# Two scheduling rules for VectorE's banks and polynomial steps, and one multiplication in place of two, in a two-block attention kernel

## The chip, the cores and the metric

One core of a Trainium2 chip (trn2). The metric is the device time of one execution in microseconds (us), lower is better. Each execution also comes with the mean clock that TensorE was granted, as a share of full speed. A run is called slow when it lies over 1.5% above the fastest of its kernel, and such runs are left out of ratios, means and clocks. Ratios are the mean time of one kernel's fast runs over that of the other's fast runs of the same rounds, so not quite the ratio of the medians quoted beside them.

## The reference

Two attention blocks over 2048 positions, 32 heads of 16 channels, laid side by side in the output. Block A attends to everything, block B to a causal window of 256.

```python
qkv = (x @ wqkv).reshape(B, S, 3, H, Dh)...          # S = 2048, H = 32, Dh = 16
scores = jnp.einsum("bhqd,bhkd->bhqk", q, k) * (Dh ** -0.5)
# block B only: scores = where(0 <= i - j < 256, scores, -1e9)
p = _softmax(scores, axis=-1)
o = jnp.einsum("bhqk,bhkd->bhqd", p, v)
return o... @ wo                                     # a and b concatenated
```

## The kernel before

The program is unrolled in Python into 743 slots. A slot is three banks of scores (three 128 x 512 tiles), which ScalarE turns into probabilities in one instruction. Two sets of three banks take turns; one bank (`op`) accumulates the values and one (`ms`) serves everything else: projections, guards, outputs and "polynomial" scores. These last are scores whose exponential VectorE computes, to take them from ScalarE: a copy of the bank (`dy`), then, for each two banks, three steps of 1024 columns.

```python
    def poly_ok(self, key):
        at = self.landed.get(key[:2] + (key[2] // 2,))
        return (at is not None and at <= self.slot and len(self.dq) < 4
                and self.slot >= self.last_poly + 1)
...
    # in poly_steps: one bank
            b = self.bank()
            ... matmul of scores into b ...
            nc.vector.tensor_copy(out=y[:, half, :], in_=b[:])          # L622
            self.queued(OP, True)
            self.closed = self.last_poly = self.slot
    ...     # after the second bank of a pair
            self.dq += [first, second, third]                           # L633, L637, L643
```

The loop over slots. `self.vec` is the time at which VectorE's queue ends by the program's own reckoning; `whole` counts the pieces of TensorE work put into the slot, and what is lacking of two is made up by `busy`, matmuls of the identity into the score bank before the scores overwrite it:

```python
        for s, sl in enumerate(slots):
            self.slot = s
            self.exps(sl)
            if self.dq and self.by(self.vec, 0.8):
                self.queued(1.22, at=0)
                self.dq.pop(0)()
            if s + 2 < len(slots):
                self.scores(slots[s + 2])
            self.values()
            ...
            self.whole = 0
            ... a guard (whole = 1), a polynomial bank (+ 1), other tasks (+ 2) ...

    def scores(self, slot):
        ...
            if b == 0 and jb.inst == 0:
                self.busy(sps[:, 0, :], 2 - self.whole)

    def busy(self, bank, n):
        for _ in range(n):
            self.nc.tensor.matmul(bank, lhsT=self.ident[:], rhs=self.junk, start=True, stop=True)
```

The last two units of block A (a unit is four heads over 512 positions) are normalised without a trip through memory: reciprocals of the sums are spread over 32 rows by matmuls with a one-row operand, then multiplied.

```python
        def spread(w):
            b = self.bank()
            for q in (slice(q, q + w) for q in range(q0, q1, w)):
                for j in range(GH):
                    r = slice(32 * j, 32 * j + 1)
                    nc.tensor.matmul(b[32 * j:32 * j + 32, q], lhsT=self.ones[r, 0:32],
                                     rhs=rec[r, q], start=True, stop=True,
                                     tile_position=(32 * j, 32 * j))         # L717
                nc.vector.tensor_mul(out=o[:, q], in0=osb[:, q], in1=b[:, q])  # L720
                self.queued(OP * w / 512, True)
```

## Time and profile before

| | before |
|---|---|
| median of the first 3 runs | 1049.49 us (1048.85 to 1050.01) |
| span of the profiled run, mean clock | 1048.8 us, 0.987 |
| ScalarE's exponentials (L590): busy, idle before them | 998.1 us, 22.3 us |
| TensorE busy | 935.5 us, 200.7 of it filler (L156) |
| half-clock stretches between the first and the last exponential | 3.4 us at 142, 10.2 us at 657, 6.8 us at 1019 |

How to read it: ScalarE has something to do in every slot, so its idle time is all that a better order can win. The prediction shows the lines.

### The profile page before, as it was taken

The numbers are of one execution on the slowest core, as the hardware profiler recorded it, in microseconds if no ns is written. First come the engines' busy times: TensorE is split into PE (matmuls) and PEld (weight loads), VectorE is DVE, ScalarE is ACT, GpSimd is POOL, SyncE is SP. The second block draws the span as 40 slices with busy tenths as digits, with TensorE's granted clock in tenths as the row PEclk, the third lists the DMA queues.
The fourth block names the chain that finished last, engine by engine and source line by source line (L and its number), as shares of the span: only waits on it lengthen the run. The fifth ranks groups of instructions, "written<-read, shape, count | busy, mean of one in ns | idle before, by whom it ended". The sixth has DMA issues, their size and how long they took to land.

```text
span 1048.8 us, 18724 instructions
## 1 busy us (share of the span) xinstructions
PE 935.5 (89%) x7653; PEld 317.6 (30%) x7653; DVE 722.3 (69%) x943; ACT 1008.3 (96%) x775; POOL 20.1 (2%) x100
## 2 busy tenths in 40 slices
PE   8888788888899989999998999999999999998887
PEld 5322222232233323333322333233222332323322
DVE  4432265537867977788788767877877768587754
ACT  5999999999999999999999999899999999999996
POOL 6000000000000000000000000000000000000000
PEclk9999999999999999999999999899999999999998
DMA  7021431112232103211230312123102211221101
GB/s 242 6 82 37 134 114 46 54 65 78 72 83 78 63 26 94 72 63 43 81 104 26 96 61 76 47 80 88 65 32 84 73 57 61 79 73 42 51 13 42
DMA packets 72359, 73.05 MB, mean 70 GB/s; under 512 B 22584, under 2 KB 55888, under 8 KB 72272
## 3 DMA queue, kind: packets, MB, share of 16 engines
q1 hardware_dynamic: 69216, 68.01, 21.0%
q0 software_dynamic: 768, 2.13, 0.5%
q10 hardware_dynamic: 2288, 1.70, 0.5%
q8 instruction: 60, 0.98, 0.4%
q14 instruction: 27, 0.22, 0.1%
HBM read 38.65 MB, written 31.07 MB: 66 GB/s over the span
## 4 chain that ended last, share of the span: by engine, by line
ACT 58%; PE 23%; issue 11%; DVE 7%; DMA 1%; ACTq 0%; DVEq 0%
ACT pT L590 58%; PE sps L563 5%; PE op L682 4%; PE ms L252 4%; PE sps L156 4%; PE ms L619 2%; PE sps L572 2%; DVE dy L622 2%; DVE dh L633 1%; DVE pD L643 1%; DMA kTa<-in_A_x_dram 1%; DVE dh L637 1%; DVE kst L270 0%; PE op L252 0%; PE sps L830 0%
## 5 line engine op out<-in xcount | busy, mean ns | idle before, releaser
L590 ACT ACTIVATE pT<-sps 128x1536 bf16<-128x1536 f32 (+3 forms) x759 | 998.1, 1470 | 22.3 <-PE sps L563 17.9
L563 PE MATMUL sps<-qTa,kTa 32*128 32x512 bf16 (+1 forms) x1904 | 248.7, 380 | 8.7 <-ACT pT L590 7.5
L156 PE MATMUL sps<-ident 128*128 128x512 bf16 x608 | 200.7, 383 | 54.7 <-ACT pT L590 47.9
L622 DVE COPY dy<-ms 128x512 f32<-128x512 f32 x204 | 139.9, 686 | 117.2 <-PE ms L619 116.4
L682 PE MATMUL op<-pT,va 128*32 128x512 bf16 (+1 forms) x1904 | 188.5, 386 | 0.8 <-ACT pT L590 0.6
L563 PEld LDWEIGHTS <-kTa 32*128 32x128 bf16 x1904 | 65.6, 91 | 237.2 <-issue 235.6
L633 DVE SCALAR_TENSOR_TENSOR dh<-dy 128x1024 f32<-128x1024 uint16 x102 | 124.6, 1222 | 2.8
L637 DVE SCALAR_TENSOR_TENSOR dh<-dy,dh 128x1024 f32<-128x1024 uint16 x102 | 124.0, 1215 | 1.5
L643 DVE SCALAR_TENSOR_TENSOR pD<-dh,dy 128x1024 uint16<-128x1024 f32 x102 | 124.0, 1216 | 1.0
L156 PEld LDWEIGHTS <-ident 128*128 128x128 bf16 x608 | 55.2, 96 | 166.5 <-issue 160.4
L619 PE MATMUL ms<-qTa,kTa 32*128 32x512 bf16 (+1 forms) x208 | 78.0, 378 | 11.2 <-DVE dy L622 2.8
L682 PEld LDWEIGHTS <-va 128*32 128x32 bf16 x2112 | 51.3, 93 | 106.1 <-issue 104.1
L572 PE MATMUL sps<-mask,ident 128*128 128x128 bf16 (+1 forms) x640 | 77.8, 248 | 0.0
L563 PE MATMUL sps<-qTb,kTb 32*128 32x384 bf16 (+2 forms) x704 | 56.1, 274 | 16.2 <-ACT pT L590 14.2
L759 DVE COPY osb<-op 128x512 f32<-128x512 f32 x62 | 42.5, 685 | 23.1 <-PE op L682 23.0
L572 PEld LDWEIGHTS <-ident 128*128 128x128 bf16 x640 | 43.6, 97 | 31.9 <-issue 29.2
L376 DVE TENSOR_SCALAR qs<-ms 128x512 bf16<-128x512 f32 x31 | 21.3, 689 | 37.8 <-PE ms L252 37.4
L270 DVE CAST kst<-ms 128x512 bf16<-128x512 f32 x28 | 19.3, 689 | 35.6 <-PE ms L252 35.2
L252 PE MATMUL ms<-wv,xT 128*128 128x368 bf16 (+2 forms) x176 | 37.7, 318 | 1.1 <-DVE qs L376 0.5
L563 PEld LDWEIGHTS <-kTb 32*128 32x128 bf16 x704 | 24.7, 92 | 42.0 <-issue 36.8
L252 PE MATMUL ms<-xT,wq 128*128 128x512 bf16 x124 | 35.4, 382 | 1.9 <-DVE dy L622 1.2
L682 PE MATMUL op<-pT,vb 128*32 128x384 bf16 (+2 forms) x704 | 36.6, 280 | 0.5 <-DVE osb L759 0.2
(105 smaller groups left out, 421.9 us busy)
## 6 DMA issues: line engine op xcount, KB each, us to landing
od<-osb SPq DMA_DIRECT2D x62, 256.0 KB
oc<-od SPq DMA_DIRECT2D x31, 256.0 KB
rb<-rd SPq DMA_DIRECT2D x31, 256.0 KB
kTb<-kd SPq DMA_DIRECT2D x16, 256.0 KB
qTb<-qd SPq DMA_DIRECT2D x16, 256.0 KB
qd<-qs SPq DMA_DIRECT2D x31, 128.0 KB
out_dram<-ob SPq DMA_DIRECT2D x31, 128.0 KB
qTa<-qd SPq DMA_DIRECT2D x15, 256.0 KB
```

The lines of the kernel that those rows point to most:

```text
L156: self.nc.tensor.matmul(bank, lhsT=self.ident[:], rhs=self.junk, start=True, stop=True)
L252: self.nc.tensor.matmul(bank, lhsT=lhs(c), rhs=rhs(c), start=(c == 0), stop=(c == NC - 1))
L563: self.nc.tensor.matmul(sps[:, b, o:o + q1 - q0], lhsT=kT[r, gg, k0:k0 + P], rhs=qT[r, gg, q0:q1], start=(o == jb.subs[0][3]), stop=not jb ...
L572: self.nc.tensor.matmul(sps[:, b, o:o + P * len(kind)], lhsT=self.ident[:], rhs=m, start=False, stop=True, skip_group_check=True)
L590: nc.scalar.activation(out=pT[:, b:e, :n], in_=sps[:, b:e, :n], func=ACT.Exp, scale=LN2 / 128, bias=-127 * LN2)
L619: nc.tensor.matmul(b[:, o:o + q1 - q0], lhsT=kT[r, g % 2, k0:k0 + P], rhs=self.qT[0, p, g // 2][r, g % 2, q0:q1], start=True, stop=True, t ...
L622: nc.vector.tensor_copy(out=y[:, half, :], in_=b[:])
L633: nc.vector.scalar_tensor_tensor(out=st["h"][:], in0=low, scalar=-65536.0, in1=low, op0=ALU.add, op1=ALU.mult)
L637: nc.vector.scalar_tensor_tensor(out=st["h"][:], in0=low, scalar=65536.0 * POLY[1], in1=st["h"][:], op0=ALU.add, op1=ALU.mult)
L643: nc.vector.scalar_tensor_tensor(out=out.bitcast(U16), in0=st["h"][:], scalar=POLY[0] * 2.0 ** -41, in1=flat, op0=ALU.mult, op1=ALU.add)
L682: self.nc.tensor.matmul(op[32 * jb.j:32 * jb.j + 32, q0:q1], lhsT=self.v[jb.inst, kt][:, h * VP:h * VP + 32], rhs=jb.pT[:, o:o + q1 - q0], ...
L759: nc.vector.tensor_copy(out=osb[:], in_=self.op[i, p, g][:])
```

## The change

The intent: banks for VectorE at least two slots apart, steps only when its queue is short, and one multiplication of 512 columns instead of two of 256 in the last unit but one.

```diff
-                and self.slot >= self.last_poly + 1)
+                and self.slot >= self.last_poly + 2)
...
                     nc.tensor.matmul(b[32 * j:32 * j + 32, q], lhsT=self.ones[r, 0:32],
                                      rhs=rec[r, q], start=True, stop=True,
                                      tile_position=(32 * j, 32 * j))
+                if self.mid:
+                    nc.vector.tensor_mul(out=o[:, q], in0=osb[:, q], in1=b[:, q])
+            if not self.mid:
+                q = slice(q0, q1)
                 nc.vector.tensor_mul(out=o[:, q], in0=osb[:, q], in1=b[:, q])
-                self.queued(OP * w / 512, True)
+                self.queued(OP, True)
...
-            if self.dq and self.by(self.vec, 0.8):
+            if self.dq and self.by(self.vec, 0.4):
```

## The prediction

> **What bounds the kernel now.** I read the page's busy shares first, then the groups of instructions, then who waited for whom, then the rows of ScalarE in order of time, and last the stretches in which ScalarE stood still.
>
> ```profile
> PE 935.5 (89%) x7653; PEld 317.6 (30%) x7653; DVE 722.3 (69%) x943; ACT 1008.3 (96%) x775; POOL 20.1 (2%) x100
> PEclk9999999999999999999999999899999999999998
> L590 ACT ACTIVATE pT<-sps 128x1536 bf16<-128x1536 f32 (+3 forms) x759 | 998.1, 1470 | 22.3 <-PE sps L563 17.9
> L156 PE MATMUL sps<-ident 128*128 128x512 bf16 x608 | 200.7, 383 | 54.7 <-ACT pT L590 47.9
> L622 DVE COPY dy<-ms 128x512 f32<-128x512 f32 x204 | 139.9, 686 | 117.2 <-PE ms L619 116.4
> L633 DVE SCALAR_TENSOR_TENSOR dh<-dy 128x1024 f32<-128x1024 uint16 x102 | 124.6, 1222 | 2.8
> ```
>
> ScalarE is the bound: the exponentials of L590 alone cover 998.1 of the 1048.8 us and wait only 22.3 us in all. The kernel runs in slots of one exponential; most start 1.33 to 1.34 us after the one before. The change takes no work from ScalarE: in the built program it has 784 instructions before and after. So everything that can be won lies in those 22.3 us, and in the head (21 us until the first exponential) and the tail (7.8 us after the last), which the change hardly touches. TensorE's 89% is padded: L156 is filler that nobody reads, put in where a slot has less than two other pieces of work.
>
> The 22.3 us, row by row in time (my sorting, by what stands just before each wait): 2.7 us in the first 56 us; 9.9 us in or just behind three stretches in which TensorE's clock was halved (1.8 at 142 us, 3.8 at 657 us, 4.4 at 1019 us); 4.6 us in 19 waits with a wait of TensorE for a bank of VectorE within 2.8 us before; 2.9 us in slots with mask matmuls; some 2 us of others. The last of the clock stretches, at the end, shows the mechanism at its largest:
>
> ```profile
> 1016.42 0.69 DVE L622 COPY dy<-ms 128x512 f32<-128x512 f32 x1 [1.62 <-PE ms L619]
> 1017.14 1.22 DVE L633 SCALAR_TENSOR_TENSOR dh<-dy 128x1024 f32<-128x1024 uint16 x1
> 1017.31 0.63 PE L717 MATMUL ms<-oc,padneg 1*32 1x256 f32 x8
> 1018.28 0.41 DVE L720 TENSOR_TENSOR oTa<-osb,ms 128x256 bf16<-128x256 f32 x1
> 1018.75 0.78 PE L717 MATMUL ms<-oc,padneg 1*32 1x256 f32 x8 [0.81 <-DVE oTa L720]
> ...
> 1020.73 1.45 ACT L590 ACTIVATE pT<-sps 128x1536 bf16<-128x1536 f32 x1 [1.96 <-PE sps L563]
> ```
>
> Columns: start, duration, engine, line; in brackets the idle time before and who ended it. The first half of the spreading matmuls (L717) is done, its multiplication stands behind a 1.22 us polynomial step, the second half waits 0.81 us for that multiplication, the scores behind it come late, and ScalarE stands for 1.96 us. Then the clock:
>
> ```profile
> 1015.70:1019.10 3.40, 2.59 (x44) 0.84 (x41) 2.25 (x3) 3.07 (x3) 0.00 (x0) 1.00 0.02 5
> 1019.10:1025.90 6.80, 6.80 (x47) 1.59 (x43) 2.75 (x4) 2.90 (x2) 0.00 (x0) 0.50 0.06 19
> ```
>
> (Stretch, length, busy time of PE, PEld, DVE, ACT, POOL, clock, DMA share, GB/s.) After a stretch with TensorE busy for 2.59 of 3.40 us, the clock is 0.50 for 6.8 us, and ScalarE is busy for only 2.90 of them.
>
> **What the Trainium skill says.** "TensorE: Matmul & The Clock Gate", section "What's actually happening": a monitor halves TensorE's clock after an idle window of about 3.4 us and restores it after a busy one. The trace agrees on the step (0.50) and the lengths (the three stretches are 3.4, 10.2 and 6.8 us); but TensorE was not idle before them, only less busy (2.40 of 3.50, 2.64 of 3.40, 2.59 of 3.40 us), and other windows as thin passed. "PSUM — Partial Sum Buffer", "PSUM bank collisions raise a hardware error": guard by bank, not by address. That is why the second half of the spread waits for the multiplication of the first, though the columns differ (0.81 us above). "VectorE: DVE Perf Modes", "The perf-mode tier table", gives an fp32 operand in PSUM one element a cycle; L622 takes 686 ns for 512, so one 512-wide multiplication should cost about what L788 takes (some 680 ns) against 0.41 + 0.42 us for two halves. The same engine's queue is in order (the TensorE page, "Architectural detail"); the trace shows it: L720 behind L633.
>
> **The change, part by part.**
>
> 1. A polynomial bank at most every second slot. The number of banks is fixed (208 matmuls of L619, 204 copies of L622, before and after), so no work goes. In the two built programs' order I counted the distances, in slots, between slots with such a bank: 53 of 203 were 1 before, none after; 2 goes from 49 to 85. Where two banks fall in neighbouring slots the second matmul, or the projection after it, waits for a 0.69 us copy that may stand behind a 1.22 us step. At 232.9, 391.8 and 868.1 us TensorE so waits 0.84, 0.85 and 0.58 us, and ScalarE then 0.74, 0.54 and 0.41 us. Of the 4.6 us in bank waits I take half, **-2.3 us**; the other half follows copies of keys, queries and outputs, which the rule does not space.
>
> 2. A polynomial step only if VectorE's modelled queue ends by 0.4 of the slot, not 0.8. It removes no instruction (306 steps of about 1.22 us). It keeps long steps from piling up before a bank's copy, but delays results. The order does not show harm: matmuls of L682 that run a slot later than usual fall from 55 to 25. I book it in part 1, **0**.
>
> 3. One multiplication after all eight spreading matmuls in the last unit but one. Saved on VectorE: 0.83 - 0.68 = 0.15 us, off the path. What counts is the 0.81 us wait in the middle of the spread, and that in the new order the multiplication stands before the polynomial step, not behind it. Without the pause the spread lasts about 1 us from 1017.31, then a filler: scores begin near 1018.6 instead of 1020.0, and ScalarE, which was ready at 1018.77, waits some 0.3 instead of 1.96 us. That is -1.4 to -1.6 us. If the window is then full enough that the clock stays up, the waits of 0.92 and 1.48 us behind it shrink too; but two groups of four output matmuls still stand in the way, so I count -3.2 us in all then. At 6 to 4 for the clock staying up: 0.6 x 3.2 + 0.4 x 1.4 = **-2.5 us**.
>
> 4. A side effect: fillers fall from 608 to 579, since slots with a bank and a projection together need none. That is 29 x 0.21 us = 6 us of TensorE time (0.21 us is the step between two fillers in the timeline). It is no gain, as TensorE isn't the bound; it makes thin windows a little likelier. The two middle clock stretches cost 5.6 us now; I add **+0.5 us**.
>
> Sum: -2.3 + 0 - 2.5 + 0.5 = -4.3 us, 1049.49 - 4.3 = **1045.2 us**.
>
> **The rivals.** (a) *Nothing moves.* ScalarE is 96% busy and each bank wait removed is met by another: the new order moves 208 banks to other slots, and some fall beside mask slots. For it speaks that only 4.6 us are at stake in the middle; against it the plain chain at 1018 us. It would give 1048 to 1049.5 us. (b) *The clock decides.* With fewer fillers a further window or two drops to half clock: 3.4 us of it cost ScalarE about 1.8 us at 142 us, 10.2 us cost 3.8. For it speaks that the count of fillers falls and TensorE's weighted work with it by 1.1%; against, that the end gets denser. Two more stretches give 1049 to 1051 us; losing the middle ones too gives 1040 us. (c) *Polynomial results come late*, the accumulation of a unit must wait for them, and VectorE's chain becomes the bound at the ends of units. The lag count (55 to 25) speaks against it; it would give 1052 us or more.
>
> **Range and chances.** The three runs of before lie within 1.2 us, so the range is that of the model: (a) at the top, the good side of (b) at the bottom: 1041.5 to 1049.3 us. Faster by over 2% needs -21 us, nearly all of the 22.3 us: 0.01. Slower by over 2% needs (c) in full: 0.01. The rest, 0.98, is within 2%.
>
> **What would show each step right or wrong.** Part 3: the eight L717 matmuls follow each other with no wait in the middle, and ScalarE's wait behind them is under 1 us. Part 1: TensorE's waits for L622 (4.4 us in 10 waits among the matmuls into these banks) fall by half or more, and L590's idle time falls from 22.3 to 16 to 19 us, L590's busy time staying within 2 us of 998. Part 4: the half-clock stretches between 100 and 1000 us number two, give or take one. The prediction is wrong if the waits for banks fall and L590's idle time does not, or if clock stretches come or go by more than one.

## The result, and the profile after

The changed kernel took 1040.97 us (median of 4 runs, 1039.03 to 1042.57), against 1049.17 us for the kernel before (4 runs): ratio 0.9921, 95% interval 0.9897 to 0.9944. That is "same" at 2%, as forecast, but twice the predicted gain and just outside the range. The page of the changed kernel:

```profile
PE 907.8 (87%) x7537; PEld 313.1 (30%) x7624; DVE 722.8 (69%) x942; ACT 1007.2 (97%) x775; POOL 20.1 (2%) x100
PEclk9999999999999999999999999999999999998999
...
L590 ACT ACTIVATE pT<-sps 128x1536 bf16<-128x1536 f32 (+3 forms) x759 | 997.0, 1486 | 15.2 <-PE sps L563 10.6
L156 PE MATMUL sps<-ident 128*128 128x512 bf16 x579 | 191.1, 382 | 60.8 <-ACT pT L590 52.2
L622 DVE COPY dy<-ms 128x512 f32<-128x512 f32 x204 | 139.9, 686 | 109.2 <-PE ms L619 107.4
```

(The trace lacks the records of 87 projection matmuls, 7537 against 7624 weight loads, so PE's 907.8 us is too low; e4_both_rules below, whose trace has them all, shows 921.4 us.)

The span is 1040.9 us, 7.9 less. L590's idle time fell by 7.1 us, from 22.3 to 15.2; its busy time by 1.1. So the gain is where it had to be. But sorting its waits as in the prediction gives: start 2.7 us as before; bank waits 4.1 (4.6 before); slots with mask matmuls 3.5 (2.9); others 2.3 (1.8); in or behind half-clock stretches 2.1 (9.9). The banks gave almost nothing; nearly all lies in and behind the clock stretches. Not all of that is the clock's own: the 1.96 us wait of the old spread is in it, of which the prediction put 1.4 to 1.6 us down to the pause in the spread. TensorE's waits for L622's banks did fall, from 4.4 to 2.7 us, but those for the copy of keys (L270) rose from 2.4 to 5.1 us, so together they did not fall. Before and after, TensorE's idle time ahead of a matmul into these banks, by who ended it (us, times):

```profile
  DVE dy L622: 4.4, 10
  DVE kst L270: 2.4, 5
...
  DVE kst L270: 5.1, 10
  DVE dy L622: 2.7, 9
```

The spread at the end, in order of time (columns as in the prediction):

```profile
1011.80 0.69 DVE L622 COPY dy<-ms 128x512 f32<-128x512 f32 x1 [1.58 <-PE ms L619]
...
1012.69 1.07 PE L717 MATMUL ms<-oc,padneg 1*32 1x256 f32 x16
...
1013.83 0.69 DVE L724 TENSOR_TENSOR oTa<-osb,ms 128x512 bf16<-128x512 f32 x1 [1.33 <-PE ms L717]
...
1014.43 1.22 DVE L633 SCALAR_TENSOR_TENSOR dh<-dy 128x1024 f32<-128x1024 uint16 x1
1014.53 2.96 ACT L590 ACTIVATE pT<-sps 128x1536 bf16<-128x1536 f32 x2 [0.37 <-PE sps L563]
```

The eight spreading matmuls (16 records) run through in 1.07 us, the multiplication stands before the polynomial step, and ScalarE waits 0.37 us instead of 1.96. The stretches around it, and around the only half-clock stretch that this profile has in the middle:

```profile
944.40:947.80 3.40, 2.26 (x31) 0.79 (x23) 3.01 (x4) 3.40 (x4) 0.00 (x0) 1.00 0.30 101
947.80:954.60 6.80, 6.80 (x38) 1.24 (x36) 3.65 (x4) 5.06 (x4) 0.00 (x0) 0.50 0.14 48
...
1011.40:1014.80 3.40, 3.25 (x45) 1.26 (x43) 1.66 (x3) 3.03 (x4) 0.00 (x0) 1.00 0.02 5
```

With the spread at 1012 us TensorE is busy for 3.25 of 3.40 us and keeps its clock. A thin window at 944 us (2.26 of 3.40) costs 6.8 us of half clock. Of the four runs, two with clocks of 0.995 and 0.997 took 1042.5 us each, two with 0.999 took 1039.0 and 1039.5 us.

**Theory:** the gain is TensorE's clock. A 3.4 us window in which the array does too little is followed by half clock; the scores come late and ScalarE waits. The change fills or moves the thin windows. **Rival:** the gain is the shorter waits for VectorE's banks, and the clock stretches of the two profiles are chance.

### The profile page after: what moved, and what is told of

The parts are those of the page before. It is cut to its first block, busy times and chain, and to the rows that moved or that the text cites. A ratio compares the mean times of both kernels' runs of the same rounds, so it can differ in the third digit from the quotient of the medians.

```text
span 1040.9 us, 18590 instructions
## 1 busy us (share of the span) xinstructions
PE 907.8 (87%) x7537; PEld 313.1 (30%) x7624; DVE 722.8 (69%) x942; ACT 1007.2 (97%) x775; POOL 20.1 (2%) x100
## 4 chain that ended last, share of the span: by engine, by line
ACT 62%; PE 18%; issue 12%; DVE 6%; DMA 1%; ACTq 0%; DVEq 0%
ACT pT L590 62%; PE sps L563 4%; PE ms L252 4%; PE op L682 3%; PE sps L156 3%; PE sps L572 2%; PE ms L619 1%; DVE dy L622 1%; DVE dh L633 1%; DMA kTa<-in_A_x_dram 1%; DVE dh L637 1%; DVE qs L376 0%; DVE ob L421 0%; DVE pD L643 0%; DVE osb L763 0%
## 5 line engine op out<-in xcount | busy, mean ns | idle before, releaser
L590 ACT ACTIVATE pT<-sps 128x1536 bf16<-128x1536 f32 (+3 forms) x759 | 997.0, 1486 | 15.2 <-PE sps L563 10.6
L156 PE MATMUL sps<-ident 128*128 128x512 bf16 x579 | 191.1, 382 | 60.8 <-ACT pT L590 52.2
L622 DVE COPY dy<-ms 128x512 f32<-128x512 f32 x204 | 139.9, 686 | 109.2 <-PE ms L619 107.4
L682 PE MATMUL op<-pT,va 128*32 128x512 bf16 (+1 forms) x1904 | 185.3, 383 | 0.0
L682 PEld LDWEIGHTS <-va 128*32 128x32 bf16 x2112 | 50.6, 93 | 105.0 <-issue 104.1
L563 PE MATMUL sps<-qTb,kTb 32*128 32x384 bf16 (+2 forms) x704 | 56.2, 273 | 17.1 <-ACT pT L590 14.2
L270 DVE CAST kst<-ms 128x512 bf16<-128x512 f32 x28 | 19.3, 690 | 38.6 <-PE ms L252 38.1
L252 PE MATMUL ms<-wv,xT 128*128 128x368 bf16 (+2 forms) x161 | 34.8, 313 | 1.9 <-DVE dy L622 0.7
L345 DVE CAST va<-ms 128x368 bf16<-128x368 f32 (+1 forms) x28 | 11.8, 441 | 32.8 <-PE ms L252 32.8
```

What stands on the lines that cost most here:

```text
L252: self.nc.tensor.matmul(bank, lhsT=lhs(c), rhs=rhs(c), start=(c == 0), stop=(c == NC - 1))
L563: self.nc.tensor.matmul(sps[:, b, o:o + q1 - q0], lhsT=kT[r, gg, k0:k0 + P], rhs=qT[r, gg, q0:q1], start=(o == jb.subs[0][3]), stop=not jb ...
L590: nc.scalar.activation(out=pT[:, b:e, :n], in_=sps[:, b:e, :n], func=ACT.Exp, scale=LN2 / 128, bias=-127 * LN2)
L682: self.nc.tensor.matmul(op[32 * jb.j:32 * jb.j + 32, q0:q1], lhsT=self.v[jb.inst, kt][:, h * VP:h * VP + 32], rhs=jb.pT[:, o:o + q1 - q0], ...
```

## The experiments

All outputs are right. "Clock" is the mean over a kernel's fast runs. The four groups of rounds had before at 1048.17, 1049.11, 1049.62 and 1049.21 us (medians of 11 runs each). Medians are over all runs: c4_few_fillers has one slow run (1106.41 us) and before in the third group another (1058.69 us); without them the medians are 1085.23 and 1049.25 us.

| run | what | median us | clock | ratio to before, 95% interval |
|---|---|---|---|---|
| e1_spacing | bank rule alone | 1049.68 | 0.9855 | 1.0023 (0.9998 to 1.0048) |
| e2_queue | queue rule alone | 1048.19 | 0.9860 | 1.0009 (0.9976 to 1.0043) |
| e3_spread | spread alone | 1045.94 | 0.9913 | 0.9990 (0.9966 to 1.0015) |
| e4_both_rules | both rules, old spread | 1043.37 | 0.9938 | 0.9958 (0.9935 to 0.9981) |
| a2_after_again | the changed kernel | 1040.40 | 0.9965 | 0.9924 (0.9883 to 0.9964) |
| c4_few_fillers | changed, fewer fillers | 1085.52 | 0.8696 | 1.0353 (1.0306 to 1.0399) |
| c2_two_holes | changed, 16 fillers out | 1046.54 | 0.9822 | 1.0000 (0.9934 to 1.0067) |
| c1_two_patches | before, 9 fillers in | 1045.46 | 0.9950 | 0.9955 (0.9936 to 0.9974) |
| d4_before_filled | before, 152 fillers in | 1053.82 | 0.9937 | 1.0049 (1.0006 to 1.0093) |
| d3_after_filled | changed, 142 fillers in | 1046.72 | 0.9983 | 0.9984 (0.9940 to 1.0028) |
| d1_loads_uncounted | changed, 12 fillers in | 1040.74 | 0.9960 | 0.9929 (0.9880 to 0.9977) |

### The parts one by one

e1_spacing: only the bank rule.

```diff
-                and self.slot >= self.last_poly + 1)
+                and self.slot >= self.last_poly + 2)
```

> The kernel before with only the bank rule (two slots apart). Clock theory (the gain of 8 us is that TensorE's clock is no longer halved at 142, 657 and 1019 us, and those stretches cost ScalarE 9.9 us of waits): the stretch at 1019 us stays, as the spread is untouched, and costs some 4 us; whether the two in the middle go depends on how full the moved slots are, so 1041 to 1050 us, and in the profile L590's idle time is 12 us plus what lies in half-clock stretches. Rival (waits for VectorE's banks are the gain): 1043 to 1045 us, with TensorE's waits for L622 well below the 4.4 us of before.

Measured: no gain (1.0023). Its profile has half clock at 301 us (3.4 us), 728 us (13.7 us) and 1018 us (6.8 us); 11 us of L590's 22.3 us of idle time lie outside them and the few us behind. TensorE's waits for L622's banks fell all the same, from 4.4 to 2.6 us, as in the changed kernel. The bank rival, which wanted 1043 to 1045 us from this rule, fails. The stretch at 728 us has a cause of its own. The windows before and in it (columns as before), and TensorE's wait in the timeline:

```profile
724.20:727.60 3.40, 1.64 (x16) 0.43 (x13) 2.95 (x4) 3.08 (x3) 0.00 (x0) 1.00 0.90 200
727.60:741.30 13.70, 12.36 (x51) 2.15 (x51) 7.85 (x10) 7.92 (x6) 0.00 (x0) 0.50 0.35 107
```

```profile
722.88 2.16 SPq L241 DMA_TRANSPOSE xT<-in_B_x_dram  x1
...
728.70 0.61 PE L252 MATMUL ms<-xT,wk 128*128 128x512 bf16 x1 [2.87 <-DMA xT<-in_B_x_dram]
```

The rule moved the projection of keys closer to the transposed load of its input: it starts 5.8 us after the load is issued, the wait included, against 8.8 us in the kernel before. TensorE waited 2.87 us for the transfer; that emptied the window. ScalarE was then busy for 7.92 of 13.70 us.

e2_queue: only the queue rule.

```diff
-            if self.dq and self.by(self.vec, 0.8):
+            if self.dq and self.by(self.vec, 0.4):
```

> The kernel before with only the tighter rule for polynomial steps (0.4 of a slot for 0.8). Clock theory: as for the run with the bank rule alone, the stretch at 1019 us stays; fillers fall from 608 to 590 but values lag less, so slots are filled more evenly: 1043 to 1048 us, half-clock stretches in the middle none or one. Bank rival: near 1049 us, as neighbouring banks stay (51 of 203 distances are 1).

Measured: no gain (1.0009), clock 0.9860, a miss for my hope that the middle would have none or one: the profile has 3.4 us at 142, 10.2 us at 667 and 3.4 us at 773, and the one at 1019 us (3.4 us). It speaks against the bank rival once more: TensorE's waits for L622's banks nearly doubled, from 4.4 to 8.4 us, and the time stayed.

e3_spread: only the third hunk of the change, the rest as before.

> The kernel before with only the multiplication after all eight spreading matmuls. The order of everything before 1008 us is the kernel before's, so the stretches at 142 and 657 us should be there again. Clock theory: the stretch at 1019 us goes, ScalarE's waits behind the spread fall from 4.4 to about 0.7 us, as in the changed kernel: 1045.3 us, -3.6. Bank rival, which counts only the 0.81 us pause and the late multiplication: -1.5 us, 1047.7 us, with the clock still at 0.50 around 1019 us.

Measured: 1045.94 us, ratio 0.9990 with an interval that includes 1, so the predicted 3.6 us are not resolved in the times; the difference of the means, -1.4 us, lies nearer to the rival's -1.5, and the mean clock (0.9913) is hardly above that of before in the same rounds (0.9905). The profile shows the point itself: no half clock around the spread, and ScalarE's waits behind it are 1.0 us, not 4.4. And it shows something that I had not expected: the order before 1008 us is that of the kernel before, yet the stretches at 142 and 657 us are not there; one at 970 us is. So where the clock drops differs from execution to execution of the same order.

e4_both_rules: both rules, the old spread.

> The changed kernel with the old spread in two halves: both scheduling rules, not the third part. Clock theory: the middle as in the changed kernel (none or one short stretch), the stretch at the end back: 1041 + 3.6 = 1044.6 us. If the parts add, this and the run of the spread alone sum to -8.2 us.

Measured: 1043.37 us, ratio 0.9958: a clear gain where each rule alone had none. Half clock at 98 us (3.4 us) and, as expected, behind the old spread at 1013 us (6.8 us). By the means this is -4.1 us, with e3_spread's -1.4 in all -5.5 where the expectation had -8.2; the intervals are too wide to say that the parts do not add.

a2_after_again: the changed kernel once more.

> The changed kernel again, to have it on the same chip and in the same rounds. Clock theory: about 1041 us, mean clock about 0.997, every run on the line 1039.1 us + 0.70 us for each 0.001 under full clock within 1 us. Against the runs of before of these rounds: some 5 to 7 us faster.

Measured: 1040.40 us, ratio 0.9924, as the first time. Its profiled execution had no half clock at all between the first and the last exponential, and took 1039.16 us.

### Is it the clock?

Every run has a time and a mean clock. For the 44 fast runs of the kernel before whose clock is listed (1042.4 to 1057.0 us, clock 0.998 to 0.979; one slow run of 1058.69 us is left out) the two correlate at -0.98. One line through these and the ten runs of the changed kernel, with one slope, gives 0.70 us for each 0.001 of mean clock (some 2.1 us at half clock), and at full clock 1041.0 us for before and 1038.4 us for after. The slope is that of before: the ten runs of the changed kernel alone, with clocks of 0.994 to 1.000, give 0.39 us and correlate at only -0.60. A line is not yet a cause, so fillers were taken out and put in.

c4_few_fillers: one filler fewer in each slot.

```diff
-                self.busy(sps[:, 0, :], 2 - self.whole)
+                self.busy(sps[:, 0, :], 1 - self.whole)
```

> The changed kernel with one filler fewer in every slot (187 for 579); all other instructions and their order the same. Clock theory, from the runs so far (a line through all runs of six kernels: 0.70 us for each 0.001 that the mean clock lies under 1, about 1039 us at full clock for the changed kernel): TensorE is thinner everywhere, the mean clock falls to 0.97 or less, and the time rises along that line, to over 1055 us. If fillers only take TensorE's time and the clock does not matter, it is equal or some us faster, 1038 to 1041 us.

Measured: 1085.52 us. From its page, the clock in 40 slices and the exponentials:

```profile
PEclk9998889897768789987899988889888999887768
...
L590 ACT ACTIVATE pT<-sps 128x1536 bf16<-128x1536 f32 (+3 forms) x759 | 1005.2, 1468 | 50.6 <-PE sps L563 38.5
```

Work that nobody reads was taken away, and the kernel lost 45 us against the changed one: L590's idle time went from 15.2 to 50.6 us. The direction is settled. The size is not on the line (0.13 under full clock would be 91 us). That half clock costs less where fewer fillers fill TensorE would explain it, but no run shows it.

c2_two_holes: fillers out in two short places.

```diff
-                self.busy(sps[:, 0, :], 2 - self.whole)
+                n = 2 - self.whole if not 353 <= self.row <= 360 and not 538 <= self.row <= 544 else 0
+                self.busy(sps[:, 0, :], n)
```

(`row` counts the calls of `scores`.)

> The changed kernel with 16 fillers taken out of 579 in two places, slots 353 to 360 (near 500 us) and 538 to 544 (near 750 us), where no run so far had a half-clock stretch. Clock theory: half-clock stretches appear at both places, each of 3.4 to 10.2 us, ScalarE waits 1 to 4 us at each, mean clock falls by 0.003 to 0.010, time rises by 2 to 7 us to 1043 to 1047 us, though TensorE has 3.4 us less to do. Without the clock theory: no change, or a little faster.

Measured: 1046.54 us, clock 0.9822 (4 runs, 1043.0 to 1056.5). The two places in its profile:

```profile
496.50:499.90 3.40, 2.21 (x20) 0.67 (x18) 2.97 (x5) 3.40 (x4) 0.00 (x0) 1.00 0.17 45
499.90:510.10 10.20, 9.03 (x52) 1.78 (x48) 6.12 (x9) 9.46 (x8) 0.00 (x0) 0.50 0.18 54
...
752.50:769.60 17.10, 16.45 (x75) 2.84 (x74) 10.56 (x12) 13.92 (x11) 0.00 (x0) 0.50 0.04 15
```

and the same two stretches of the unpatched changed kernel (a2_after_again):

```profile
499.90:510.10 10.20, 9.34 (x78) 3.05 (x77) 7.02 (x12) 10.20 (x8) 0.00 (x0) 1.00 0.20 64
...
752.50:769.60 17.10, 15.12 (x108) 4.39 (x107) 14.62 (x16) 17.10 (x14) 0.00 (x0) 1.00 0.00 1
```

Half clock came at the two holes, 10.2 and 17.1 us long, and ScalarE lost 0.7 and 3.2 us in them, while with the fillers it was busy throughout. (17.1 us is longer than I had expected.) The place near 500 us is a weaker witness: d1_loads_uncounted, below, has 6.8 us of half clock there without a hole. Near 752 to 769 us no other trace has half clock, c4_few_fillers aside. The fair comparison in time is that d1, in the same rounds, took 1040.8 us (mean) at a clock of 0.9960; c2's four runs have a mean of 1048.2 us at 0.9822.

c1_two_patches: the kernel before, nine fillers more in two places where its traces had half clock.

```diff
-                self.busy(sps[:, 0, :], 2 - self.whole)
+                n = 2 - self.whole + (self.row in (85, 86, 87, 88, 465, 466, 467, 468, 469, 470))
+                self.busy(sps[:, 0, :], n)
```

> The kernel before with nine fillers more (617 for 608), in slots 85 to 88 and 465 to 470, where its half-clock stretches at 142 us and at 656 us (two of three traces, 10.2 us each) begin. Clock theory: both places stay at full clock; with 656 us tripping in some two of three executions, the mean half-clock time falls by about 7 us, the mean clock rises by 0.003 and the time falls by some 2 us against before of the same rounds. If the place does not matter, the time is that of before.

Measured: 1045.46 us, ratio 0.9955, clock 0.9950 against 0.9876 for before in the same rounds. Both places keep their clock in its one profile (which has 3.4 us each at 129, 231 and 1017 us):

```profile
138.40:145.30 6.90, 6.42 (x42) 1.97 (x41) 4.81 (x7) 6.70 (x6) 0.00 (x0) 1.00 0.38 124
650.00:667.50 17.50, 16.47 (x135) 5.13 (x131) 15.80 (x19) 17.28 (x14) 0.00 (x0) 1.00 0.21 69
```

Nine matmuls that compute nothing won 4.2 us (by the means), as much as both scheduling rules together. No bank, step or spread was moved. So the clock alone can give what the rules gave. That is twice what I had expected (some 2 us and 0.003 of clock, measured 0.0074): more than the two places account for, and why is open. That the rules themselves work through the clock rests on e1 and e2, where waits for banks fell or doubled and the time stayed, and on e4_both_rules's clock (0.9938 against 0.9905 for before, by the slope 2.4 of its 4.1 us).

### More fillers everywhere

d4_before_filled and d3_after_filled: fillers also in slots whose task only starts a transfer, and one more after a slot without values.

```diff
-        self.whole += 1 if t["name"][0] == "d" else 2
+        self.whole += {"d": 1, "w": 0, "x": 0, "wo": 0, "ends": 0}.get(t["name"][0], 2)
...
-                self.busy(sps[:, 0, :], 2 - self.whole)
+                self.busy(sps[:, 0, :], 2 - self.whole + (self.valued < self.slot))
```

(`valued` is the slot after the last one with values.)

> The kernel before, its schedule of banks, polynomial steps and spread untouched, with fillers where it skipped them for nothing: tasks that only start a transfer no longer count as TensorE work, and a slot whose values group was empty gets one filler more (760 for 608). Clock theory: the mean clock rises to 0.995 or more and the time falls to 1041 to 1044 us, most of the change's gain without the change; the stretch at the end, behind the old spread, stays in most runs. If the change's gain is its own scheduling, it stays at 1048 us or gets slower by up to the 152 x 0.21 = 32 us of added TensorE work where that does not fit.

> The changed kernel with the same two filler rules (721 for 579). Clock theory: clock 0.998 or more in all runs, 1039 to 1040 us, a little faster than the changed kernel and with less spread; if the added 142 x 0.21 = 30 us of TensorE work do not fit into its waits, some us slower at a high clock.

Measured: both miss. The clock did rise, from 0.989 to 0.994 and from 0.997 to 0.998, but the times rose too, to 1053.82 and 1046.72 us. The page of d3_after_filled has full clock, and yet the exponentials are busy for longer and wait longer than in a2_after_again (996.3 and 14.1 us there):

```profile
PE 933.0 (89%) x7679; PEld 318.6 (30%) x7766; DVE 722.6 (69%) x942; ACT 1010.7 (97%) x775; POOL 20.1 (2%) x100
PEclk9999999999999999999999999999999999999999
...
L591 ACT ACTIVATE pT<-sps 128x1536 bf16<-128x1536 f32 (+3 forms) x759 | 1000.6, 1452 | 17.1 <-PE sps L564 11.2
```

Fillers are not free where a slot is full already. Taken to full clock by the slope, d3 is some 7.1 us above the changed kernel for 142 fillers, d4 some 8.2 us above before for 152: about 0.05 us each, an estimate from these means. Few in the right place help; many everywhere cost.

d1_loads_uncounted: the first of the two filler rules alone, on the changed kernel.

> The changed kernel with only this rule: a task that does nothing but start transfers (weights, inputs, the last rows of wo) no longer counts as TensorE work, so that its slot gets its fillers (591 for 579). It aims at the one half-clock stretch in the profile of the changed kernel (947.8 us), which begins just after the task that loads the last rows of wo. Clock theory: that place no longer trips, mean clock 0.998 or more, 1039 to 1040 us, about 1 us under the changed kernel. If twelve fillers are too little to tell: 1040.5 us, as the changed kernel.

Measured: 1040.74 us, clock 0.9960: no difference from the changed kernel. In its profile the stretch at 948 us is gone, and one of 6.8 us stands at 500 us. So the place at 948 us was mended and the clock did not gain: the expected 0.998 was missed. No version beat the changed kernel clearly.

### Second and third traces

b2_before_look and b3_before_look: the kernel before, unchanged, one look each.

> The kernel before, unchanged, for a second trace of it. Clock theory with windows that run free of the kernel: the half-clock stretches are not at 142 and 657 us again but at other thin places (or some of the same), while the one at 1015 to 1026 us, behind the spread, comes again in most executions. If they belong to fixed places of the program: 142, 657 and 1019 us again, to 2 us.

> The kernel before, unchanged, for a third trace, with the same expectations as the second: by the clock theory, other middle places than in the first two traces, and a stretch near 1019 us in most.

Measured (single runs, state unknown): 1044.04 us with half clock at 358 us (3.4) and 1014 us (3.4); 1047.92 us with 390 us (3.4), 656 us (10.2) and 1018 us (3.4). So over three traces of one program: behind the spread each time, near 656 us in two, the rest at changing places. Both extremes of the expectation were wrong: some places are likely, none certain but the spread.

e1_look2, e2_look2 and e4_look2: second traces of the parts.

> The bank rule alone, a second trace. If it trips at places of its own making, the stretch of 13.7 us at 728 us comes again; if its low clock was chance, the middle has 3 to 10 us of half clock, at other places.

> The queue rule alone, a second trace. It left slots 465 to 470 nearly as before, so a stretch near 655 to 667 us should come again; 141 and 773 us may not.

> Both rules with the old spread, a second trace: no stretch near 656 or 728 us, at most 7 us of half clock in the middle, and a stretch at 1012 to 1020 us again.

Measured (single runs): e1_look2 1051.60 us, again 13.7 us of half clock at 730 us behind a wait of 3.0 us for the same transfer, and 3.4 us at 129, 6.8 at 975 and 6.8 at 1020 us. e2_look2 1049.65 us, with 13.7 us at 129 us, 3.4 us each at 235 and 269 us, 6.8 us at 538 us behind a wait of 1.7 us for the input of the same kind, 3.4 us at 661 us, and none behind the spread. (e2_queue has such a wait of 1.8 us at 532 us and kept its clock there.) e4_look2 1042.15 us, three of 3.4 us (129, 300 and 1013 us), none near 656 or 728 us.

This suggests why neither rule helps alone. Near 656 us two of before's three traces trip (e3_spread's, in the same order, does not), and those of the queue rule alone at 661 and 667 us; none of the nine traces with the bank rule does, c4_few_fillers left out. But the bank rule alone puts the projection close behind its load near 728 us. With both rules it starts 7.4 us after the load is issued and does not wait, and neither place trips in four traces (two each of e4 and the changed kernel). So few traces make this likely, not shown. In e1, e2 and no other kernel does TensorE wait over 1.5 us for the load of block B's input. That the two rules fit together looks like chance of a scheduler that takes whatever task fits next; no run tested it.

## Why the prediction was wrong

The class was right (within 2%), and so was the bound: the gain came out of ScalarE's 22.3 us of idle time. The size was half of what was measured.

- **Part 1, -2.3 us from bank waits: failed.** Half of 4.6 us was to go; 0.5 us did. Waits for L622's banks fell (4.4 to 2.7 us), waits for the copy of keys rose (2.4 to 5.1 us). That is rival (a), and it was right for this part.
- **Part 2, 0:** alone it is 0 (e2_queue); together with part 1 the two are worth some 4 us (e4_both_rules), 2.4 of them through the clock by the slope.
- **Part 3, -2.5 us: right in mechanism, its size not settled.** No pause in the spread, ScalarE's wait 0.37 us, clock up there. Of eleven traces with the old spread and near-normal fillers (three of before, e1, e2 and e4 twice each, c1, d4) ten have half clock behind it; of six with the new one (e3, d1, d3, c2, two of the changed kernel) one has. In the times, the changed kernel's two ratios (0.9921, 0.9924) lie some 0.0035 under e4_both_rules's, 3.7 us, but from other rounds; e3_spread alone gives -1.4 us, not resolved.
- **Part 4, +0.5 us: the step that failed worst.** It said that the two middle clock stretches stay and that fewer fillers make thin windows likelier. (Its sign, two stretches between 100 and 1000 us, give or take one, was met by the first profile, which has one, and failed in a2_after_again's, which has none.) The mean clock rose, from 0.9892 (44 runs of before) to 0.9969 (10 runs of after): 7.7 x 0.70 = 5.4 us of the 7.9 us between the means (1048.5 and 1040.6). I had counted fillers in all, where what counts is the thinnest 3.4 us. "It is no gain" was wrong too: fillers that do not fit cost about 0.05 us each, so 29 fewer may be worth 1.5 us, an estimate from d3 and d4. The remaining 1 us or so may be the pause in the spread itself: taken to full clock by the same slope, e3_spread, which has the new spread and all fillers, lies 1.0 us under before. This too is an estimate.
- **The range:** "The three runs of before lie within 1.2 us, so the range is that of the model" failed. Three runs happened to agree; 44 lie between 1042.4 and 1057.0 us. Rival (b) named what decides, the clock, but I gave its good side only the bottom of the range.

What stays open: which of the thin windows trip in a given execution, and whether the two rules' fit could be had on purpose.

## What to carry to other kernels

When an engine with a clock that follows activity feeds the bound, look at the thinnest few microseconds of its work, not at its mean: nine useless matmuls in the right slots did as much as two scheduling rules, and 150 spread out did harm. Read the mean clock beside every time before comparing two schedules, and take more than three runs, since one program's clock differs from execution to execution. And a task that only starts a transfer, or stands two slots in front of its consumer, can empty such a window.

## What the Trainium skill lacked or had wrong

- "TensorE: Matmul & The Clock Gate", "HAM oscillation — how this bites in real kernels", gives as the rule that TensorE must not idle for over 3.4 us. Here the longest idle time within the window before the stretch at 948 us is 0.95 us, and TensorE was busy for 2.26 of 3.40 us; half clock came all the same.
- The same page, "What's actually happening", says busy-ness sets the clock and, but for a remark on transposes, not what counts as busy. Add up, from the matmul records, each one's columns times the share of the 128 x 128 array that its tile uses, in windows of 3.413 us (fillers alone, 512 columns each 0.21 us, would give some 8000). In the 18 traces all 75 windows just before a half-clock stretch (33 of them in c4_few_fillers) were under 3250, and 133 of the other 5123 windows at full clock. Busy time separates far worse: one of the 75, in c2_two_holes at 1015 us, was busy for 3.26 us, and 3804 of the others were busy for no longer. So a matmul on 32 rows seems to count a quarter, and a spread with one row next to nothing. This is a fit to these traces, not a test of its own; five of them lack 75 to 87 projection matmuls each, and it does not say which thin window trips (in before one of 2658, at 121 us, kept full clock).
- The same section has full clock come back after at least one busy window of about 3.4 us, and does not say how long that takes in practice; here half-clock stretches are 1 to 7 windows long (3.4 to 23.9 us, the longest in c4_few_fillers). In the stretch at 1019 us of before TensorE was busy for 6.80 of 6.80 us and got full clock back only at the end.
- No page gives the price: on this kernel 0.70 us for each 0.001 of mean clock, and a spread of 1042.4 to 1057.0 us over 44 runs of one program.
- "VectorE: DVE Perf Modes", "The perf-mode tier table", on which part 3 leaned, was not wrong: one 512-column multiplication with a PSUM operand took 0.69 us, two of 256 took 0.41 and 0.42 us.
